# Attention with two feed-forward layers on one core: the probabilities of units 6 to 17 transposed by VectorE instead of TensorE

## The chip, the core and the metric

One core of a Trainium2 chip runs the whole program. The rows call the engines PE (TensorE's matmuls), PEld (its weight loads), DVE (VectorE), ACT (ScalarE), POOL (GpSimd) and SP (SyncE, which issues the DMAs here). The metric is the device time of one execution in microseconds; the time of a kernel is the median of its runs.

## The reference

Local attention over chunks of 64 tokens (8 batches, 8 heads, 576 tokens, head size 64), and two feed-forward layers on the 4608 tokens that come out:

```
scores = q_c @ k_c^T / 8                  # per head and chunk: 64 x 64
attn   = softmax(scores)
out    = attn @ v_c                       # then laid out as x: 4608 x 512
h      = (x @ w1) * (x @ w2) @ w3
y      = h @ w_out                        # 4608 x 512
g      = y @ w_in;  g = max(g,0) + alpha*min(g,0)
result = g @ w_out2                       # 4608 x 512
```

Everything is float32 on the outside. Inside, the large matmuls run in a 32-bit format with fewer bits (fp32r): each operand is split into a high and a low half, and three matmuls (`mm3`) replace one.

## The kernel before

The 4608 tokens are 9 blocks `b` of 512. A **unit** `u` is the attention of 256 tokens, so two units make the x of one block: 18 units. Four steps make a unit: `attn_scores` with `attn_max` and `attn_exp` (TensorE, VectorE, ScalarE); `attn_softmax` (VectorE scales the exponentials `e`); `attn_transpose` and `attn_copy` (TensorE transposes eight 128 x 128 tiles of `e` into the PSUM tile `pa`, ScalarE copies them to `pt` in SBUF); `attn_values` and `attn_out` (TensorE multiplies by the values, again into `pa`, and ScalarE and VectorE split the result into the halves of x).

The program has these stages. In the *first* the units 0 to 5, the conversion of the weights and the first projections of three blocks run in an order written out as a table. In the *second*, 24 steps `proj_wc` for blocks 0 to 2 follow each other, one per `f` of 8 and block: 12 matmuls `acc<-gs,wc` each, for which `load_g` fetches a product `g` from DRAM and VectorE and ScalarE split it into `gs` (three buffers). Units 6 and 7 are put between the steps by the dictionary `todo`. At the last `f` of a block `empty_pair` copies the accumulators to `y` (VectorE and ScalarE in turn) and stores them. In the *third*, blocks 3 to 8 are worked through in eight columns `f` each: `proj1` into bank `a`, `proj1` into bank `b`, and `proj_wc` of the column before into `acc`, 12 matmuls each. ScalarE copies `a` out of its bank, and VectorE's `product` (rows a<-b,a) multiplies it with bank `b`; the split makes `gs`. There is one bank of each kind. In blocks 3 to 7 the two units of the next block are put between the columns, a first unit at f = 0 to 3 and a second at 4 to 7; in blocks 3 to 6 a piece of the weights of the last stage is converted too (rows with m, p, raw, wm). The *last* stage, the second feed-forward layer, takes the rest of the time.

TensorE's order is the program's order in all stages. In the second and third stage the order on VectorE and ScalarE is set by a scheduler from the order of the code and from its own estimates.

Of the kernel before, what the change touches and what calls it, by code (L numbers as in the profile page):

```python
# [10 lines left out]
F32 = mybir.dt.float32  # L11
# [6 lines left out]
P = 128  # L18
# [34 lines left out]
LEAD = 3  # L53
# [6 lines left out]
def tile_attention_moe_moe(ctx: ExitStack, tc: tile.TileContext, qkv: bass.AP, w12: bass.AP,  # L60
# [14 lines left out]
    D = 64  # L75
# [7 lines left out]
    work = ctx.enter_context(tc.tile_pool(name="work", bufs=2))  # L83
# [25 lines left out]
    pe, act, dve = InOrder(nc.tensor), InOrder(nc.scalar), InOrder(nc.vector)  # L109
# [6 lines left out]
    def tmp(name):  # L116
        return work.tile([P, TB], F32, tag="tmp", name=name, bufs=TMP)
# [9 lines left out]
    def bank(which):  # L127
        return psum.tile([P, TB], F32, tag=which, name=which, bufs=1)

    def pair(which, name):  # L130
        return psum.tile([P, 2, TB], F32, tag=which, name=name, bufs=1)
# [64 lines left out]
    def convert():  # L196

        i = ahead[0]
        if i < len(conv):
            convert_a(i)  # L200
            convert_b(i)
            convert_c(i)
            convert_a(i + 1)
            convert_d(i)
            convert_e(i)
            ahead[0] = i + 1

    def w2_load(f):
        for half in range(2):
            g = w2_g[f, half] = granule(2 * f + half, "w2")  # L210
            nc.sync.dma_start(out=g.bitcast(F32), in_=w2_dram[f, half])
# [10 lines left out]
    un = {}  # L222
# [12 lines left out]
    def load_unit(u):  # L235
        unit_tiles(u)
        load_qk(u)
        load_v(u)
# [16 lines left out]
    def attn_scores(u, where="att"):  # L255
        s = un[u]["s"] = pair(where, "sc")
        for j in range(2):
            q, k = (un[u]["qk"][j][:, i].rearrange("p (a c s) -> p a c s", a=4, c=2) for i in range(2))
            for a in range(4):
                for h2 in range(2):  # L260
                    for c in range(2):
                        r0, c0, to = D * h2, D * c, (4 * j + a) * D
                        pe.matmul(s[c0:c0 + D, h2, to:to + D], q[r0:r0 + D, a, c], k[r0:r0 + D, a, c],
                                         start=True, stop=True)

    def attn_max(u):
        mx = un[u]["mx"] = small.tile([P, 2, 8], F32, tag="mx", name="mx")
        dve.tensor_reduce(out=mx, in_=un[u]["s"].rearrange("p h (a k) -> p h a k", k=D), axis=AX.X, op=ALU.max)
        dve.tensor_scalar_mul(mx, mx, -SCALE)

    def attn_exp(u, tiles=range(2)):
        mx, s, e = un[u]["mx"], un[u]["s"], un[u]["e"]
        if tiles[0] == 0:
            un[u]["sm"] = small.tile([P, 2, 4, 2], F32, tag="sm", name="sm")
        sm = un[u]["sm"]
        for j in tiles:
            for a in range(4):
                for h2 in range(2):
                    n, h = 4 * j + a, h2 ^ (a & 1 if u >= CROSS else 0)
                    act.activation(out=e[:, j, a, h], in_=s[:, h2, n * D:(n + 1) * D], func=AF.Exp,  # L280
                                         bias=mx[:, h2, n:n + 1], scale=SCALE, accum_out=sm[:, j, a, h:h + 1])

    def attn_softmax(u):
        e, sm = un[u]["e"].rearrange("p j a h k -> p (j a h) k"), un[u].pop("sm").rearrange("p j a h -> p (j a h)")
        dve.tensor_scalar_add(sm, sm, 1e-9)
        dve.reciprocal(sm, sm)
        dve.tensor_tensor(out=e, in0=e, in1=sm.unsqueeze(2).to_broadcast([P, 16, D]), op=ALU.mult)

    def attn_transpose(u, where="att"):
        e = un[u]["e"]  # L290
        pa = un[u]["pa"] = pair(where, "pa")
        for j in range(2):
            for a in range(4):
                pe.transpose(pa[:, j, a * P:(a + 1) * P], e[:, j, a].rearrange("p h k -> p (h k)"), ident)

    def attn_copy(u):
        pt = un[u]["pt"] = work.tile([P, 2, 4, 2, D], F32, tag="pt", name="pt", bufs=1)
        act.copy(pt.rearrange("p j a c s -> p j (a c s)"), un[u]["pa"])

    def attn_values(u):  # L300
        v, pt = un[u]["v"].rearrange("p j a (c d) -> p j a c d", c=2), un[u]["pt"]
        xo = un[u]["pa"].rearrange("p o (i j c s) -> p o i j c s", i=2, j=2, c=2)
        for j in range(2):
            for c in range(2):
                for i in range(2):
                    for odd in range(2):
                        for h2 in range(2):
                            a, h = 2 * i + odd, h2 ^ (odd if u >= CROSS else 0)
                            r, to = slice(D * h, D * h + D), slice(D * h2, D * h2 + D)
                            pe.matmul(xo[to, odd, i, j, c], v[r, j, a, c], pt[r, j, a, c], start=True, stop=True)  # L310

    def attn_out(u, lo):
        b, i = divmod(u, 2)
        if not lo and i == 0:
            x_t[b] = work.tile([P, 2, KD, TB], F32R, tag="x", name="x", bufs=2)
        xs = [x_t[b][:, s].rearrange("p (i o) t -> p o i t", o=2)[:, :, :, 2 * P * i:2 * P * (i + 1)] for s in (HI, LO)]
        pa = un[u]["pa"].rearrange("p o (i t) -> p o i t", i=2)
        if lo:
            dve.tensor_tensor(out=xs[LO], in0=pa, in1=xs[HI].bitcast(F32), op=ALU.subtract)
            un.pop(u)  # L320
        else:
            act.copy(xs[HI], pa)
# [23 lines left out]
    def proj1(b, f, which, ps):  # L346
        w = w_g["a", f, which].rearrange("p s (k c) -> p s k c", k=KD)
        for k in range(KD):
            mm3(ps, lambda s: w[:, s, k], lambda m: x_t[b][:, m, k], k == 0, k == KD - 1)

    def product(b, f, a, ps):
        dve.tensor_tensor(out=a, in0=ps, in1=a, op=ALU.mult)
        if b < LEAD:
            nc.sync.dma_start(out=g_dram[b, f], in_=a)
        else:
            split_g(b, f, a)
# [27 lines left out]
    def load_y(b, i):  # L384
        if i == 0:
            x_t[b, 2] = work.tile([P, 2, KD, TB], F32R, tag="x", name="y", bufs=2)
        raw = work.tile([P, 2, TB], F32, tag="raw", name="yraw", bufs=RAW)
        nc.sync.dma_start(out=raw, in_=y_dram[b][:, 2 * i:2 * i + 2])
        split(x_t[b, 2][:, :, 2 * i:2 * i + 2], raw)
# [33 lines left out]
    for step in STARTUP.split():  # L423
# [20 lines left out]
        elif kind == "k":  # L444
            a = ab[tuple(rest)][2] = tmp("a")
# [3 lines left out]
        elif kind == "m":  # L449
            _, ps, a = ab.pop(tuple(rest))  # L450
# [9 lines left out]
    def unit_steps(u, cut):  # L460


        def first():
            attn_scores(u)
            attn_max(u)
            attn_exp(u, range(1 if cut else 2))

        def second():
            if cut:
                attn_exp(u, range(1, 2))  # L470
            attn_softmax(u)
            if u + 1 < NU:
                load_unit(u + 1)

        def third():
            attn_transpose(u)
            attn_copy(u)

        def fourth():
            attn_values(u)  # L480
            attn_out(u, False)
            attn_out(u, True)
        return [first, second, third, fourth]
# [4 lines left out]
    load_unit(2 * LEAD)  # L488
    todo = {}
    for i in range(2):  # L490
        for at, part in zip((1, 3, 7, 9), unit_steps(2 * LEAD + i, True)):
            todo[10 * i + at] = part
    for n, (b, f) in enumerate(steps):
        if n + 2 < len(steps):
# [7 lines left out]
    for b in range(LEAD, NB):  # L502
        parts = [p for i in range(2) for p in unit_steps(2 * (b + 1) + i, False)] if b + 1 < NB else []
        for f in range(NF1):
            if parts and f % 4 == 1:
                parts[4 * (f // 4) + 1]()
            pa, pb = bank("a"), bank("b")
            proj1(b, f, 0, pa)
            a = tmp("a")
            act.copy(a, pa)  # L510
            if parts and f % 4 == 0:
                parts[4 * (f // 4)]()
            if parts and f % 4 == 2:
                parts[4 * (f // 4) + 2]()
            proj1(b, f, 1, pb)
            product(b, f, a, pb)
            if parts and f % 4 == 2:
                parts[4 * (f // 4) + 3]()
            if b < NB - 2:
                convert()  # L520
            if b == NB - 1:
                if f < 4:
                    w2_load(f)
                w2_load(4 + f)
                if f in (3, 6):
                    load_y(0, f // 3 - 1)
            proj_wc(*pend)
            pend = b, f
# [62 lines left out]
```

## Time and profile before

| | |
|---|---|
| median of 3 runs | 1518.82 us (1518.38 to 1521.39) |
| profiled execution | 1517.93 us, span 1516.2 us |
| TensorE busy | 1489.0 us, 98% of the span |
| VectorE busy | 792.7 us, 52% |
| ScalarE busy | 420.8 us, 28% |
| granted clock of TensorE | 1.00 throughout |

The second stage runs from about 224 to 298 us of the span, the third from there to about 805 us. A row of the timeline has its start, its length and, in brackets, how long the engine was idle before it and what ended that. Starts of successive rows of an engine say more than lengths, since instructions overlap.

### The profile page before, as it was taken

The numbers are of one execution on the slowest core, as the hardware profiler recorded it, in microseconds if no ns is written. First come the engines' busy times: TensorE is split into PE (matmuls) and PEld (weight loads), VectorE is DVE, ScalarE is ACT, GpSimd is POOL, SyncE is SP. The second block draws the span as 40 slices with busy tenths as digits, with TensorE's granted clock in tenths as the row PEclk, the third lists the DMA queues.
The fourth block names the chain that finished last, engine by engine and source line by source line (L and its number), as shares of the span: only waits on it lengthen the run. The fifth ranks groups of instructions, "written<-read, shape, count | busy, mean of one in ns | idle before, by whom it ended". The sixth has DMA issues, their size and how long they took to land.

```text
span 1516.2 us, 21102 instructions
## 1 busy us (share of the span) xinstructions
PE 1489.0 (98%) x8688; PEld 1228.1 (81%) x8688; DVE 792.7 (52%) x1250; ACT 420.8 (28%) x1108; POOL 0.7 (0%) x6
## 2 busy tenths in 40 slices
PE   5999999999999999999999999999999999999998
PEld 5778887788888888888888888888888888888887
DVE  7998983376666664221434343443434344343433
ACT  6553334344444443321111111111111111111111
POOL 0000000000000000000000000000000000000000
PEclk9999999999999999999999999999999999999999
DMA  8544457255555545156301010010101000000000
GB/s 304 164 139 151 148 165 224 87 198 166 182 183 175 181 163 185 43 166 195 112 0 56 0 43 14 3 53 1 56 0 56 1 14 28 1 28 0 29 1 28
DMA packets 61712, 141.89 MB, mean 94 GB/s; under 512 B 6576, under 2 KB 20912, under 8 KB 61616
## 3 DMA queue, kind: packets, MB, share of 16 engines
q1 hardware_dynamic: 61616, 140.54, 27.9%
q8 instruction: 68, 1.11, 0.3%
q14 instruction: 28, 0.23, 0.0%
HBM read 98.57 MB, written 41.94 MB: 93 GB/s over the span
## 4 chain that ended last, share of the span: by engine, by line
PE 90%; DVE 5%; ACT 2%; DMA 1%; issue 1%; SPq 0%; DVEq 0%; ACTq 0%
PE acc L104 38%; PE b L104 23%; PE a L104 22%; PE ab L104 2%; DVE m L104 2%; PE pa L104 2%; PE wc L104 2%; ACT e L104 1%; DVE p L104 1%; PE sc L104 1%; DMA g<-g_dram 1%; DMA raw<-in_w 0%; DVE a L104 0%; DVE e L104 0%; DVE w L104 0%
## 5 line engine op out<-in xcount | busy, mean ns | idle before, releaser
L104 PE MATMUL acc<-w,gs 128*128 128x512 f32 x1728 | 414.7, 389 | 0.0
L104 PEld LDWEIGHTS acc<-w,gs 128*128 128x128 f32 x1728 | 324.6, 188 | 67.0
L104 ACT CAST gs<-g 128x512 fp32r<-128x512 f32 x168 | 104.5, 622 | 661.3 <-DVE g L104 635.0
L104 PE MATMUL acc<-gs,wc 128*128 128x512 f32 x864 | 208.8, 393 | 3.1 <-DVE gs L104 3.0
L104 PE MATMUL a<-y,w 128*128 128x512 f32 x864 | 207.5, 389 | 0.0
L104 PE MATMUL b<-y,w 128*128 128x512 f32 x864 | 207.5, 389 | 0.0
L104 PEld LDWEIGHTS acc<-gs,wc 128*128 128x128 f32 x864 | 160.5, 188 | 39.3 <-DVE gs L104 4.2
L104 PEld LDWEIGHTS a<-y,w 128*128 128x128 f32 x864 | 162.3, 188 | 33.6
L104 PEld LDWEIGHTS b<-y,w 128*128 128x128 f32 x864 | 162.3, 188 | 33.6
L104 DVE TENSOR_TENSOR gs<-g,gs 128x512 fp32r<-128x512 f32 x168 | 116.2, 692 | 132.8 <-ACT gs L104 132.6
L104 PE MATMUL b<-x,wa 128*128 128x512 f32 x720 | 175.7, 393 | 0.1
L104 PE MATMUL a<-x,wa 128*128 128x512 f32 x720 | 173.5, 390 | 1.4 <-DVE x L104 1.4
L104 PEld LDWEIGHTS a<-x,wa 128*128 128x128 f32 x720 | 134.9, 188 | 29.6 <-DVE x L104 1.6
L104 PEld LDWEIGHTS b<-x,wa 128*128 128x128 f32 x720 | 133.6, 188 | 28.0 <-DVE wa L104 0.5
L104 DVE TENSOR_SCALAR g<-b,alpha_sb 128x512 f32<-128x512 f32 x72 | 54.0, 750 | 178.0 <-PE b L104 178.0
L104 DVE TENSOR_SCALAR g<-a,alpha_sb 128x512 f32<-128x512 f32 x72 | 54.0, 751 | 162.3 <-PE a L104 162.3
L104 ACT ACTIVATE e<-sc,mx 128x64 f32<-128x64 f32 x288 | 85.7, 354 | 29.0 <-DVE mx L104 28.9
L104 DVE TENSOR_SCALAR m<-m 128x512 f32<-128x512 f32 (+1 forms) x144 | 60.9, 424 | 59.9 <-ACT m L104 58.3
L104 DVE TENSOR_TENSOR a<-b,a 128x512 f32<-128x512 f32 x60 | 41.3, 688 | 88.1 <-PE b L104 84.0
L104 ACT COPY a<-a 128x512 f32<-128x512 f32 x60 | 35.9, 599 | 138.7 <-PE a L104 119.9
L104 PE MATMUL ab<-x,wa 128*128 128x512 f32 x288 | 68.4, 392 | 2.7 <-ACT a L104 2.7
L104 ACT ACTIVATION_READ_ACCUMULATOR e<-sc,mx 128x1 f32 x288 | 70.5, 248 | 0.0
(55 smaller groups left out, 978.6 us busy)
## 6 DMA issues: line engine op xcount, KB each, us to landing
qk<-in_qkv SPq DMA_DIRECT2D x36, 512.0 KB, 6.2
raw<-in_w2nd SPq DMA_DIRECT2D x32, 512.0 KB, 4.1
w_dram<-wm SPq DMA_DIRECT2D x32, 512.0 KB, 3.2
w<-w_dram SPq DMA_DIRECT2D x32, 512.0 KB, 4.3
y_dram<-y SPq DMA_DIRECT2D x36, 256.0 KB, 3.0
yraw<-y_dram SPq DMA_DIRECT2D x18, 512.0 KB, 4.3
out<-o SPq DMA_DIRECT2D x36, 256.0 KB, 2.1
raw<-in_w SPq DMA_DIRECT2D x16, 512.0 KB, 4.2
```

Of the source, the lines that this page charges most:

```text
L104: ins = op(*args, **kw)
```

## The change

From unit 6 on, `attn_transpose` and `attn_copy` are replaced by `attn_transpose_blocks`: 16 VectorE transposes of 32 partitions by 8 x 32 elements each, from `e` straight into `pt`. Each turns eight 32 x 32 blocks and places them in the partition group where `attn_values` reads them. `pa` is now used by the values alone. In the second stage the third part moves from step 7 to 4 (and 17 to 14). In the third stage it moves from after `a` of column 2 to the start of column 1, right behind the scaling, and the values move from the end of column 2 to after `a` of column 3 (in the second unit from 6 to 7).

```diff
+    def attn_transpose_blocks(u):
+
+        e = un[u]["e"]
+        un[u]["pa"] = pair("att", "pa")
+        pt = un[u]["pt"] = work.tile([P, 2, 4, 2, D], F32, tag="pt", name="pt", bufs=1)
+        B = D // 2
+        for c in range(2):
+            for i in range(2):
+                for h in range(2):
+                    for k in range(2):
+                        r, to = B * (2 * c + i), B * (2 * h + k)
+                        dve.transpose(out=pt[to:to + B, :, :, c, B * i:B * i + B].rearrange("p j a s -> p (j a) s"),
+                                      in_=e[r:r + B, :, :, h, B * k:B * k + B].rearrange("p j a s -> p (j a) s"))
...
         def third():
-            attn_transpose(u)
-            attn_copy(u)
+            attn_transpose_blocks(u)
...
-        for at, part in zip((1, 3, 7, 9), unit_steps(2 * LEAD + i, True)):
+        for at, part in zip((1, 3, 4, 9), unit_steps(2 * LEAD + i, True)):
             todo[10 * i + at] = part
...
             if parts and f % 4 == 1:
                 parts[4 * (f // 4) + 1]()
+                parts[4 * (f // 4) + 2]()
             pa, pb = bank("a"), bank("b")
             proj1(b, f, 0, pa)
             a = tmp("a")
             act.copy(a, pa)
             if parts and f % 4 == 0:
                 parts[4 * (f // 4)]()
-            if parts and f % 4 == 2:
-                parts[4 * (f // 4) + 2]()
+            if parts and f % 4 == 3:
+                parts[4 * (f // 4) + 3]()
             proj1(b, f, 1, pb)
             product(b, f, a, pb)
-            if parts and f % 4 == 2:
-                parts[4 * (f // 4) + 3]()
```

On TensorE, from column 2 of a block of the third stage on (sc are the scores, pa<-ident,e the transposes, pa<-pt,v the values), before:

```order
L104 MATMUL a<-x,wa 128x512 x12
L104 MATMUL pa<-ident,e 128x128 x8
L104 MATMUL b<-x,wa 128x512 x12
L104 MATMUL pa<-pt,v 64x64 x32
L104 MATMUL acc<-gs,wc 128x512 x12
L104 MATMUL a<-x,wa 128x512 x12
L104 MATMUL b<-x,wa 128x512 x12
L104 MATMUL acc<-gs,wc 128x512 x12
L104 MATMUL a<-x,wa 128x512 x12
L104 MATMUL sc<-qk 64x64 x32
```

and now:

```order
L104 MATMUL a<-x,wa 128x512 x12
L104 MATMUL b<-x,wa 128x512 x12
L104 MATMUL acc<-gs,wc 128x512 x12
L104 MATMUL a<-x,wa 128x512 x12
L104 MATMUL pa<-pt,v 64x64 x32
L104 MATMUL b<-x,wa 128x512 x12
L104 MATMUL acc<-gs,wc 128x512 x12
L104 MATMUL a<-x,wa 128x512 x12
L104 MATMUL sc<-qk 64x64 x32
```

The transposes are gone, and the values stand one column later, between `a` and `b`.

On VectorE, at the first unit of block 5, from the scaling of `e` on, before:

```order
L104 TENSOR_TENSOR e<-e,sm 128x1024
L104 TENSOR_SCALAR p<-m 128x512
L104 TENSOR_SCALAR m<-m 128x512
L104 SCALAR_TENSOR_TENSOR p<-raw,p 128x512
L104 TENSOR_TENSOR a<-b,a 128x512
L104 TENSOR_TENSOR m<-m,wm 128x512
L104 TENSOR_SCALAR m<-m 128x512
L104 TENSOR_TENSOR gs<-a,gs 128x512
```

and now:

```order
L104 TENSOR_TENSOR e<-e,sm 128x1024
L104 TENSOR_SCALAR p<-m 128x512
L104 STREAM_TRANSPOSE pt<-e 32x8x32 x16
L104 TENSOR_TENSOR a<-b,a 128x512
L104 SCALAR_TENSOR_TENSOR p<-raw,p 128x512
L104 TENSOR_TENSOR m<-m,wm 128x512
L104 TENSOR_TENSOR gs<-a,gs 128x512
```

The 16 transposes stand ahead of the product a<-b,a, and two convert steps that stood ahead of it moved behind it.

On VectorE, at unit 7 in the second stage, before:

```order
L104 TENSOR_TENSOR e<-e,sm 128x1024
L104 TENSOR_TENSOR gs<-g,gs 128x512 x2
L104 COPY y<-acc 128x512 x2
L104 TENSOR_TENSOR gs<-g,gs 128x512 x4
L104 TENSOR_TENSOR x<-pa,x 128x2x2x256
```

and now:

```order
L104 TENSOR_TENSOR e<-e,sm 128x1024
L104 TENSOR_TENSOR gs<-g,gs 128x512
L104 STREAM_TRANSPOSE pt<-e 32x8x32 x16
L104 TENSOR_TENSOR gs<-g,gs 128x512
L104 COPY y<-acc 128x512 x2
L104 TENSOR_TENSOR gs<-g,gs 128x512 x4
L104 TENSOR_TENSOR x<-pa,x 128x2x2x256
```

The transposes stand ahead of one `gs` and of the two copies that empty the accumulators.

## Rows read from the trace of the kernel before

**Rows 1.** The page's busy times and shares of the span.
```profile
PE 1489.0 (98%) x8688; PEld 1228.1 (81%) x8688; DVE 792.7 (52%) x1250; ACT 420.8 (28%) x1108; POOL 0.7 (0%) x6
```

**Rows 2.** Stretches: length, PE, PEld, DVE, ACT, POOL, clock, DMA share, GB/s.
```profile
200.00:300.00 100.00, 97.18 (x664) 78.32 (x663) 47.74 (x77) 37.11 (x108) 0.00 (x0) 1.00 0.54 169
400.00:500.00 100.00, 100.00 (x746) 82.38 (x745) 66.12 (x118) 45.38 (x148) 0.00 (x0) 1.00 0.52 172
```

**Rows 3.** Waits of PE after 200 us: total, times, longest.
```profile
PE acc L104 <- DVE gs L104: 3.0, 3, 1.8
```

**Rows 4.** Groups by line and form: busy us, mean ns of one.
```profile
L104 DVE TENSOR_TENSOR a<-b,a 128x512 f32<-128x512 f32 x60 | 41.3, 688 | 88.1 <-PE b L104 84.0 <-issue 4.2
...
L104 PE MATMUL pa<-ident,e 128*128 128x128 f32 x144 | 19.5, 282 | 4.3 <-DVE e L104 4.3
L104 ACT COPY pt<-pa 128x1024 f32<-128x1024 f32 x18 | 18.4, 1020 | 8.1 <-PE pa L104 8.0
```

**Rows 5.** Timeline of PE, block 4: four starts of bank a.
```profile
387.85 2.89 PE L104 MATMUL a<-x,wa 128*128 128x512 f32 x12
...
398.22 2.88 PE L104 MATMUL a<-x,wa 128*128 128x512 f32 x12
...
406.38 2.88 PE L104 MATMUL a<-x,wa 128*128 128x512 f32 x12
...
415.86 2.88 PE L104 MATMUL a<-x,wa 128*128 128x512 f32 x12
```

**Rows 6.** Timeline of DVE, block 3: successive convert steps.
```profile
347.92 0.42 DVE L104 TENSOR_SCALAR m<-m 128x512 f32<-128x512 f32 x1
348.26 0.69 DVE L104 SCALAR_TENSOR_TENSOR p<-raw,p 128x512 f32<-128x512 uint32 x1
348.86 0.69 DVE L104 TENSOR_TENSOR m<-m,wm 128x512 f32<-128x512 f32 x1
```

**Rows 7.** Timeline, block 5, first unit.
```profile
455.45 1.22 DVE L104 TENSOR_TENSOR e<-e,sm 128x1024 f32<-128x1024 f32 x1
...
456.58 0.42 DVE L104 TENSOR_SCALAR p<-m 128x512 uint32<-128x512 uint32 x1
456.99 0.43 DVE L104 TENSOR_SCALAR m<-m 128x512 f32<-128x512 f32 x1
...
462.92 1.03 PE L104 MATMUL pa<-ident,e 128*128 128x128 f32 x8
```

**Rows 8.** Timeline, block 4, second unit: first row behind scaling and gs.
```profile
419.94 0.42 DVE L104 TENSOR_SCALAR p<-m 128x512 uint32<-128x512 uint32 x1
...
426.74 1.03 PE L104 MATMUL pa<-ident,e 128*128 128x128 f32 x8
```

**Rows 9.** Timeline, block 3, first unit.
```profile
313.37 0.43 DVE L104 TENSOR_SCALAR m<-m 128x512 f32<-128x512 f32 x1
...
318.23 1.03 PE L104 MATMUL pa<-ident,e 128*128 128x128 f32 x8
```

**Rows 10.** Timeline, second stage, unit 6.
```profile
238.63 0.69 DVE L104 TENSOR_TENSOR gs<-g,gs 128x512 fp32r<-128x512 f32 x1
...
244.57 1.03 PE L104 MATMUL pa<-ident,e 128*128 128x128 f32 x8
```

**Rows 11.** Timeline, second stage, unit 7.
```profile
269.74 0.69 DVE L104 TENSOR_TENSOR gs<-g,gs 128x512 fp32r<-128x512 f32 x1
...
275.06 0.59 ACT L104 COPY y<-acc 128x512 f32<-128x512 f32 x1 [0.77 <-DVE y L104]
276.05 4.97 SPq L371 DMA_DIRECT2D g<-g_dram  x6
...
282.81 3.01 PE L104 MATMUL acc<-gs,wc 128*128 128x512 f32 x12 [1.81 <-DVE gs L104]
```

**Rows 12.** Timeline, block 7, first unit.
```profile
599.20 1.22 DVE L104 TENSOR_TENSOR e<-e,sm 128x1024 f32<-128x1024 f32 x1
...
607.61 1.03 PE L104 MATMUL pa<-ident,e 128*128 128x128 f32 x8
```

## The prediction

> **What bounds the kernel now.** I read the page first. TensorE is busy for 1489.0 of 1516.2 us, VectorE for just over half of the span [rows 1]. In the stretches, TensorE is full from 300 us on at a granted clock of 1.00 (the upper level, 2.4 GHz), while VectorE is 66% busy in 400 to 500 us; only between 200 and 300 us does TensorE have gaps, 2.8 us of them [rows 2]. The waits of TensorE after 200 us agree: one kind is left, the halves `gs` from VectorE, 3.0 us in three places [rows 3]. So in the third stage each instruction taken from TensorE shortens the kernel by its time, as long as VectorE goes on delivering in time. The forecast therefore needs three things: what the transposes take on TensorE, what they take on VectorE, and how late VectorE may be at each place where they now stand.
>
> **Taken from TensorE.** Eight transposes for each of 12 units; the list's row holds 144 for 18 units, at 282 ns each [rows 4], but those overlap, so I take starts in the timeline. A column of the third stage (a, b, acc: 36 matmuls) lasts 406.38 - 398.22 = 8.16 us; one with scores between a and b lasts 415.86 - 406.38 = 9.48; one with transposes and values lasts 398.22 - 387.85 = 10.37 [rows 5]. The values are 64 matmuls of the scores' shape and will now stand where the scores stand, between a and b, so I price them like the scores: the transposes of a unit are 10.37 - 9.48 = 0.89 us. Ten units of the third stage give 8.9 us. The copy pt<-pa, 18 times 1.02 us [rows 4], leaves ScalarE, which TensorE did not wait for there; I count it at nothing, and if ScalarE were the limit it would be a further gain.
>
> **Added to VectorE.** 16 instructions per unit, each of 32 partitions by 256 elements. No such operation is in the trace. Neighbours: an instruction that takes 512 elements in 256 steps lasts 0.42 us and the next begins 0.34 us after it; one of 512 steps lasts 0.69 and the next begins after 0.60 [rows 6]. So 256 steps without a wait between them come every 0.34 us: the lower bound, 5.4 us a unit. If neighbours don't overlap, 0.42 us: 6.7 us a unit, the upper bound. An operation that turns a 32 by 32 block can't put out its first row before 32 elements came in; from 512 to 1024 elements the distance grows from 0.60 [rows 6] to 456.58 - 455.45 = 1.13 us [rows 7], 1.04 ns an element, so up to 0.03 us more than the lower bound. I take **0.36 us, D = 5.76 us a unit**, near the lower end because 15 of the 16 wait for nothing. The rest of this part is worked out in D, since everything hangs on it.
>
> The Trainium skill, "VectorE: DVE Perf Modes", section "The DRAIN you can't avoid", says that the next operation doesn't start until the pipe of the one before is empty, and its rules advise a small number of instructions. Rows 6 show starts closer than durations, by 0.08 to 0.09 us, so this trace doesn't agree for those kinds; by that rule D would be the upper bound.
>
> **What waits behind them, third stage.** VectorE works in order. Behind the 16 transposes stands the product a<-b,a of the unit's second column, which frees bank b for the next column. It lasts 0.69 us [rows 4], and I add 0.06 for the signal, an assumption, so it must begin 0.75 us before TensorE wants bank b.
> - First unit of a block (blocks 4 to 6): the transposes begin where a convert step began at 456.99; TensorE, with no transposes of its own, wants the bank at 462.92, the end of a [rows 7]. Room: 5.93 - 0.75 = 5.18 us.
> - First unit of block 3: VectorE gets there later against TensorE: 318.23 - 313.37 - 0.75 = 4.11 us [rows 9].
> - Second unit (blocks 3 to 6): 426.74 - 419.94 - 0.75 = 6.05 us [rows 8].
> - Block 7 has no conversion: the scaling begins at 599.20 and its successor 1.13 later, the bank is due at 607.61 [rows 12]: 6.53 us; the second unit is looser.
>
> With D = 5.76 TensorE waits 1.65 us in block 3, and 0.58 three times: 3.4 us together; the second units and block 7 wait for nothing. Behind the product stand convert steps and the next `gs`, with about 1 us of room, and they move together with the late TensorE. Third stage: -8.9 + 3.4 = **-5.5 us**.
>
> **What waits behind them, second stage.** Units 6 and 7 stand among steps of 12 matmuls, 2.72 us each, where VectorE must deliver one `gs` per step. Here a burst of 5.8 us covers two steps.
> - Unit 6: the last `gs` ahead of the burst begins at 238.63, so the burst runs from 239.23 to 244.99 and the `gs` behind it is usable 0.75 later, 245.74. It is due where unit 6's own transposes stood before, at 244.57 [rows 10]. The step waits 1.17 us; the 0.89 us of those transposes fall away: **+0.28 us**.
> - Unit 7: the `gs` at 269.74, then the burst from 270.34 to 276.10, one more `gs`, and only then the copies y<-acc that empty the accumulators of block 1. The first begins at 276.70, VectorE's second 0.60 later and ends at 277.99, and ScalarE's last, 0.03 behind it and 0.59 long, at 278.61, where before it ended at 275.06 + 0.59 = 275.65 [rows 11]. SyncE issues the stores of these copies and, queued behind them, the loads of g (276.05); the wait of 1.81 us for `gs` at 282.81 comes from those loads [rows 11]. So the whole chain moves by 2.96 us, and the transposes taken away ahead of it only lengthen that wait: **+2.96 us**, with no credit.
>
> Second stage: +3.2 us. Sum: -5.5 + 3.2 = **-2.3 us**. The profiled execution took 1517.93 us (span 1516.2 and 1.7 around it), 0.9 under the median of 1518.82. From the median: **1516.5 us**. In D (second stage, gain, block 3, three first units, four second units, block 7): 5.4 gives 2.5 - 8.9 + 1.3 + 0.7 = -4.4; 6.1 gives about 0; 6.4 gives +3.0; 6.72 gives 5.2 - 8.9 + 2.6 + 4.6 + 2.7 + 0.2 = +6.4.
>
> About 0.2%, 3 us, is what a measurement of this kernel can tell from no change. That is D below 5.6 for faster, above 6.4 for slower.
>
> **The rivals.**
> - *The gain stays* (chance 0.33). The transposes come every 0.34 us or less. For it: 15 of 16 have no wait, and rows 6 have this distance. Then -4.4 us, 1514.4; if moreover the copies y<-acc of unit 7 are not held up (2.6 us), 1512.
> - *The late product* (0.29), on the other side. If a transpose costs 0.40 us or more, every unit with conversion makes TensorE wait for bank b: at 0.42 us 1.5 us in each first unit, 0.7 in each second, 2.6 in block 3, and 5.2 in the second stage: 1518.8 + 6.4 = 1525.2. The change turns at 0.38 us. For it: durations without overlap, and nothing in the trace shows how this operation overlaps with itself. Against it: all other kinds do overlap. The rule of the Trainium skill's VectorE page named above gives this case.
> - *Two steps per element* (within the 0.29, 0.04 of it): 0.60 us as for the 512-step rows, D = 9.6: 10.9 - 8.9 + 5.5 + 13.3 + 14.2 + 6 = +41 us, 1560. Outside the range.
>
> The Trainium skill's "Vector Engine (DVE) Microarchitecture Reference", section 3.8, says that the transposing front end sustains one element per cycle and lane; no run here shows it yet, and it speaks against the last case.
>
> **How the numbers follow.** The forecast, a result within 3 us of before, has 0.38, the two others 0.33 and 0.29. Faster 0.33, same 0.38, slower 0.29. The range goes from 1512 (gain stays and no hold-up in unit 7) to 1526 (the upper bound of 0.42 us and a little): outside are the case of 0.60 us, 0.04, prices between 0.43 and 0.60, some 0.07, and a gain above 7 us, some 0.07. The likeliest case's own range is 1515.8 to 1521.8, two sides of 1518.8.
>
> **What would show it.** Right: the column with the values lasts 9.5 us; transposes 0.35 to 0.37 us apart; TensorE waits for VectorE's a in the first units only, 0.6 us (block 3: 1.6), and for the copies y<-acc near 275 us some 3 us; the wait behind them is still there. Wrong: no waits on bank b (then D is below 5.2 or the scaling ends earlier), waits in second units too (D above 6.05), or TensorE waiting for x at a block's start: in the second unit the values now end only 5.44 us (b and acc) ahead of the next block's a, and x<-pa,x stands behind some 4.7 us of convert steps; I left it some 1.5 us of room, the thinnest place of the working.

## The result and the profile after

The changed kernel takes 1536.98 us (median of 4 runs, 1535.05 to 1538.32) against 1518.6 for the kernel before beside it: ratio 1.0116, 95% interval 1.0104 to 1.0128. It is 18.4 us slower, outside the range of the forecast and beyond its slower rival. The profiled execution took 1536.36 us with a span of 1534.6.

The page's busy times, which answer to [rows 1]:

```profile
PE 1487.7 (97%) x8592; PEld 1221.4 (80%) x8592; DVE 869.7 (57%) x1442; ACT 408.7 (27%) x1096; POOL 0.7 (0%) x6
```

The stretches, in the columns of [rows 2]:

```profile
200.00:300.00 100.00, 91.97 (x619) 73.60 (x618) 60.52 (x108) 35.18 (x106) 0.00 (x0) 0.95 0.54 169
300.00:400.00 100.00, 96.15 (x715) 78.19 (x713) 77.20 (x151) 41.33 (x143) 0.00 (x0) 1.00 0.48 158
400.00:500.00 100.00, 94.92 (x759) 76.67 (x758) 82.43 (x159) 39.35 (x116) 0.00 (x0) 0.98 0.52 171
500.00:600.00 100.00, 95.32 (x685) 77.07 (x687) 81.23 (x160) 41.48 (x141) 0.00 (x0) 0.98 0.47 155
```

TensorE has lost its 96 transposes and is nevertheless longer under way: it is no longer full between 200 and 600 us, and its granted clock is below 1.00 in three of the four stretches. TensorE's waits after 200 us (total, times, longest), against the one row of [rows 3]:

```profile
PE b L104 <- DVE a L104: 14.3, 9, 2.9
PE acc L104 <- ACT y L104: 5.2, 1, 5.2
PE acc L104 <- DVE gs L104: 3.0, 2, 2.7
```

The first two rows are new: bank b, which VectorE's product must free, nine times, and the accumulators, once. The reason stands in one row of the groups (busy us, mean ns of one, idle before):

```profile
L104 DVE STREAM_TRANSPOSE pt<-e 32x256 f32<-32x256 f32 x192 | 83.6, 436 | 2.5
```

and in the timeline of block 5's first unit, the place of [rows 7]:

```profile
469.75 0.42 DVE L104 TENSOR_SCALAR p<-m 128x512 uint32<-128x512 uint32 x1
470.09 7.18 DVE L104 STREAM_TRANSPOSE pt<-e 32x256 f32<-32x256 f32 x16
...
473.42 2.88 PE L104 MATMUL a<-x,wa 128*128 128x512 f32 x12
477.30 0.69 DVE L104 TENSOR_TENSOR a<-b,a 128x512 f32<-128x512 f32 x1
...
478.05 3.02 PE L104 MATMUL b<-x,wa 128*128 128x512 f32 x12 [1.75 <-DVE a L104]
...
480.91 2.88 PE L104 MATMUL acc<-gs,wc 128*128 128x512 f32 x12
```

From the first of 16 transposes to the end of the last are 7.18 us, so they come (7.18 - 0.436) / 15 = 0.450 us apart, more than their own length of 0.436: they don't overlap at all. The product behind them begins at 477.30, and TensorE, which had ended a, gets bank b at 478.05. The row says 1.75 us of waiting. Counted in starts it is more: a to b 478.05 - 473.42 = 4.63 where 2.72 would do, and b to acc 2.86 instead of 2.72, 2.05 us in all. The other waits for bank b cost 0.29 to 0.33 us beside what their rows say too, apart from two behind which the clock was down.

The second stage, unit 7, the place of [rows 11]:

```profile
272.81 0.68 DVE L104 TENSOR_TENSOR gs<-g,gs 128x512 fp32r<-128x512 f32 x1
273.41 7.17 DVE L104 STREAM_TRANSPOSE pt<-e 32x256 f32<-32x256 f32 x16
...
280.61 0.69 DVE L104 TENSOR_TENSOR gs<-g,gs 128x512 fp32r<-128x512 f32 x1
281.22 1.28 DVE L104 COPY y<-acc 128x512 f32<-128x512 f32 x2
...
282.58 10.21 PE L104 MATMUL acc<-gs,wc 128*128 128x512 f32 x36 [5.21 <-ACT y L104]
283.92 3.05 SPq L385 DMA_DIRECT2D g<-g_dram  x6
```

The copies y<-acc stand behind the burst, TensorE waits for empty accumulators, and the loads of g come after that. Around this wait the clock is down (length, PE busy and matmuls, clock, DMA share, GB/s):

```profile
276.00:280.00 4.00, 1.36 (x7) 0.94 0.00 0
280.00:284.00 4.00, 1.42 (x3) 0.50 0.32 115
284.00:288.00 4.00, 4.00 (x14) 0.71 1.04 255
288.00:292.00 4.00, 4.00 (x20) 1.00 0.78 289
```

A clock of 0.50 is the lower of the two levels, 1.2 GHz; in the slice after it, at 0.71 in the mean, TensorE is busy throughout and gets through 14 matmuls in 4 us, against 20 at 1.00.

The starts of the third stage's first projection and of the last stage's, before and then now:

```profile
297.86 2.88 PE L104 MATMUL a<-x,wa 128*128 128x512 f32 x12
728.17 2.88 PE L104 MATMUL a<-y,w 128*128 128x512 f32 x12
```

```profile
304.83 2.88 PE L104 MATMUL a<-x,wa 128*128 128x512 f32 x12
746.60 2.88 PE L104 MATMUL a<-y,w 128*128 128x512 f32 x12
```

So the third stage ended near 728 us before, not near 805 as said above; nothing in the argument hangs on that. Up to the third stage 7.0 us were lost, 0.3 of them before the second stage began. The third stage lasts 441.77 us instead of 430.31, 11.5 more. The last stage lasts 788.0 us in both.

### The profile page after: what moved, and what is told of

The parts are those of the page before. It is cut to its first block, busy times and chain, and to the rows that moved or that the text cites. A ratio compares the mean times of both kernels' runs of the same rounds, so it can differ in the third digit from the quotient of the medians.

```text
span 1534.6 us, 21067 instructions
## 1 busy us (share of the span) xinstructions
PE 1487.7 (97%) x8592; PEld 1221.4 (80%) x8592; DVE 869.7 (57%) x1442; ACT 408.7 (27%) x1096; POOL 0.7 (0%) x6
## 4 chain that ended last, share of the span: by engine, by line
PE 73%; DVE 15%; ACT 5%; DMA 3%; issue 2%; SPq 1%; ACTq 0%; DVEq 0%
PE acc L104 32%; PE b L104 18%; PE a L104 17%; DVE pt L104 5%; ACT e L104 4%; DVE m L104 3%; PE ab L104 2%; DVE p L104 2%; PE wc L104 2%; PE pa L104 1%; DVE mx L104 1%; DVE e L104 1%; DMA v<-in_qkv 1%; DVE a L104 1%; DVE gs L104 1%
## 5 line engine op out<-in xcount | busy, mean ns | idle before, releaser
L104 PEld LDWEIGHTS acc<-gs,wc 128*128 128x128 f32 x864 | 163.8, 191 | 45.3 <-ACT y L104 6.1
L104 PE MATMUL b<-x,wa 128*128 128x512 f32 x720 | 180.4, 400 | 14.5 <-DVE a L104 14.3
L104 DVE STREAM_TRANSPOSE pt<-e 32x256 f32<-32x256 f32 x192 | 83.6, 436 | 2.5
L104 ACT ACTIVATION_READ_ACCUMULATOR e<-sc,mx 128x1 f32 x288 | 70.5, 248 | 0.0
```

What stands on the lines that cost most here:

```text
L104: ins = op(*args, **kw)
```

## Experiments

The theory: the transposes cost 0.45 us instead of 0.36, and the two places where a whole burst stands ahead of something that TensorE needs, product and accumulator copies, turn that into waits. Rivals: the later values make x late; VectorE has simply too much to do; or the loss of one stage drives the other.

**The values' new place alone.** TensorE transposes as before, the values move to column 3:

```diff
                 parts[4 * (f // 4) + 2]()
+            if parts and f % 4 == 3:
+                parts[4 * (f // 4) + 3]()
             proj1(b, f, 1, pb)
             product(b, f, a, pb)
-            if parts and f % 4 == 2:
-                parts[4 * (f // 4) + 3]()
```

> The kernel before, with TensorE's transposes kept at column 2 of the third stage and only the values and the split of x moved to after a of column 3. Theory (the loss is VectorE's burst of 16 transposes, 0.45 us apart where 0.36 was taken): no change, 1518.6 within 2 us, no wait of TensorE for x at a block's start. Rival (the later values make x late for the next block, four or five blocks by 1 to 2 us each): 1522 to 1528, with waits of bank a for x.

Measured: 1519.3 us, ratio 1.0001 (0.9992 to 1.001). No wait for x and none for bank b, and the third stage lasts 430.32 us as before. The new place costs nothing.

**One stage at a time.** First the third stage only, with units 6 and 7 at their old steps, then the second stage only (the condition turned, and the third stage's order as before):

```diff
         def third():
-            attn_transpose_blocks(u)
+            if cut:
+                attn_transpose(u)
+                attn_copy(u)
+            else:
+                attn_transpose_blocks(u)
```

> The changed kernel, with units 6 and 7 in the second stage transposed by TensorE as before. Theory (two separate losses, one of about 7 us in the second stage, one of about 11 in the third, by the starts of block 3 in the two traces, 304.83 against 297.86): about 1530, block 3 begins at 297.9, the nine waits for bank b stay. Rival (the loss of the second stage drives the third, by what it shifts): 1519 or below.

Measured: 1527.44 us, ratio 1.0051 (1.0036 to 1.0066), with nine waits for bank b, 13.0 us together. Nearer the theory's 1530 than the rival's 1519.

> The kernel before, with only units 6 and 7 in the second stage transposed by VectorE. Theory: about 1525.6 (7.0 us later at block 3, nothing after it). Rival (the loss is all in the third stage and the second's is made up behind it): 1518.6.

Measured: 1525.13 us, ratio 1.0039 (1.0026 to 1.0051); the third stage begins at 305.18 and is undisturbed. So each stage loses by itself, 9.2 and 6.9 us. Their sum is 2.3 us short of 18.4. In the profiles the missing part lies in the third stage: alone it has one clock drop and waits of 1.73 or 1.74 us in the first units of blocks 4 to 6, in the changed kernel two drops and 2.35, 1.75 and 2.70. Whether the late second stage causes this was not tried.

**Four wide transposes instead of sixteen.** The placing across partition groups is left out:

```diff
-        for c in range(2):
-            for i in range(2):
...
+        for h in range(2):
+            for k in range(2):
+                dve.transpose(out=pt[:, :, :, h, B * k:B * k + B].rearrange("p j a s -> p (j a) s"),
+                              in_=e[:, :, :, h, B * k:B * k + B].rearrange("p j a s -> p (j a) s"))
```

> The changed kernel with 4 transposes of 128 partitions in place of 16 of 32; each turns its blocks within their own partition group, so the probabilities go to wrong places: the placing across partition groups is left out. Same elements per partition and instruction. Theory (the price is per instruction, the same 0.45 us, so a unit's burst is 1.8 us and inside every room): all waits for bank b vanish, the gain of 8.9 us in the third stage and about 0.9 in the second remain: 1508.8, from 1507 to 1511. Rival 1 (the price goes by partitions or elements in all, 1.8 us an instruction): 1537 as the changed kernel. Rival 2 (the transposes on TensorE were covered by something else, and taking them away gives nothing): 1518.

Measured: 1508.01 us, ratio 0.9924 (0.9909 to 0.9939). In the timeline of VectorE, first unit of block 5:

```profile
450.46 1.41 DVE L104 STREAM_TRANSPOSE pt<-e 128x256 f32<-128x256 f32 x4
451.80 0.65 DVE L104 TENSOR_TENSOR a<-b,a 128x512 f32<-128x512 f32 x1
```

The burst is 1.41 us, no wait for bank b or for y is left, and 10.2 us are gained. The third stage lasts 421.37 us (from 295.04 to 716.41), 8.9 less than before, which is what the prediction took from TensorE; the rest lies in the second stage. So the time taken from TensorE was sized right, and all of it is to be had. Unexpected: these four are (451.80 - 450.46) / 4 = 0.335 us apart, not 0.45. The price per instruction isn't the same.

**The same work, spread out.** All 16 transposes, units 6 and 7 by TensorE, but in four groups:

```diff
                 parts[4 * (f // 4) + 1]()
-                parts[4 * (f // 4) + 2]()
+                parts[4 * (f // 4) + 2]((0,))
+            if parts and f % 4 == 2:
+                parts[4 * (f // 4) + 2]((2,))
...
             product(b, f, a, pb)
+            if parts and f % 4 in (1, 2):
+                parts[4 * (f // 4) + 2]((2 * (f % 4) - 1,))
```

> Third stage of the change with the same 16 transposes per unit, issued as four groups of four (start of column 1, behind its product, start of column 2, behind its product); units 6 and 7 by TensorE as before. In VectorE's order 4 (first unit) or 6 (second unit) transposes now stand ahead of the product a<-b,a in place of 16. Theory (the loss is where the burst stands, 1.8 or 2.7 us against rooms of 4.1 to 6): no wait for bank b, the whole gain of 8.9 us: 1509.3, from 1508 to 1511. Rival (the loss is VectorE's total of 7.2 us more per unit, so it falls behind wherever the transposes stand): 1517 to 1527, with waits for bank b, for gs or for x.

Measured: 1512.73 us, ratio 0.9961 (0.9949 to 0.9974), with a profiled execution of 1510.29. No wait for bank b; one for x, 0.55 us. The median lies above the expected 1508 to 1511.

**One call moved.** The transposes are issued behind the product of column 1 instead of ahead of it, all 16 at once; the scheduler puts 3 or 6 of them ahead of the product by itself:

```diff
                 parts[4 * (f // 4) + 1]()
-                parts[4 * (f // 4) + 2]()
...
             product(b, f, a, pb)
+            if parts and f % 4 == 1:
+                parts[4 * (f // 4) + 2]()
```

> As the changed kernel in the third stage with one call moved: the transposes are issued behind the product of column 1 and not ahead of it; units 6 and 7 by TensorE. The scheduler puts 3 (first unit) or 6 (second unit) ahead of the product, 3 more ahead of the next gs, the rest behind. Theory: as with four groups, 1509.3, from 1508 to 1511, since neither product nor gs is late. Rival (total load): 1517 to 1527.

Measured: 1509.08 us, ratio 0.9939 (0.9926 to 0.9952): the best version that computes the reference, and faster than both kernels. In VectorE's order, first unit of block 5:

```profile
452.21 0.42 DVE L104 TENSOR_SCALAR p<-m 128x512 uint32<-128x512 uint32 x1
452.55 1.32 DVE L104 STREAM_TRANSPOSE pt<-e 32x256 f32<-32x256 f32 x3
453.90 0.69 DVE L104 TENSOR_TENSOR a<-b,a 128x512 f32<-128x512 f32 x1
454.62 1.33 DVE L104 STREAM_TRANSPOSE pt<-e 32x256 f32<-32x256 f32 x3
455.99 0.69 DVE L104 TENSOR_TENSOR gs<-a,gs 128x512 fp32r<-128x512 f32 x1
456.71 4.53 DVE L104 STREAM_TRANSPOSE pt<-e 32x256 f32<-32x256 f32 x10
```

TensorE waits for neither bank b nor x in the third stage, although VectorE is fuller than in the changed kernel (77 and 82% in these stretches):

```profile
300.00:400.00 100.00, 100.00 (x791) 81.95 (x784) 89.02 (x174) 45.99 (x151) 0.00 (x0) 1.00 0.53 175
400.00:500.00 100.00, 100.00 (x734) 82.07 (x732) 86.00 (x167) 43.19 (x145) 0.00 (x0) 1.00 0.53 173
```

The same instructions at the same price gain 9.0 us or lose 9.2, by what stands ahead of what. The rival of too much work on VectorE falls.

**Spread in the second stage too**, a group at each of steps 4 to 7 and 14 to 17:

```diff
+        for q in range(4):
+            todo[10 * i + 4 + q] = lambda third=parts[2], q=q: third((q,))
```

> The four groups in the third stage, and in the second stage too, one group at each of steps 4 to 7 and 14 to 17. Theory: unit 6 gains its 0.9 us; at unit 7 about 8 transposes still stand ahead of the copies y<-acc, which are 1.5 to 2 us late, and the loads of g behind them too: 1509.3 - 0.9 + 1.7 = 1510.1, from 1508 to 1512, not better than leaving units 6 and 7 to TensorE. Rival (spread transposes cost nothing there either): 1507.5.

Measured: 1512.15 us, ratio 0.9963 (0.9948 to 0.9978), not to be told from 1512.73. TensorE waits for the copies y<-acc in both blocks:

```profile
250.36 3.02 PE L104 MATMUL acc<-gs,wc 128*128 128x512 f32 x12 [2.54 <-ACT y L104]
...
277.17 5.73 PE L104 MATMUL acc<-gs,wc 128*128 128x512 f32 x24 [1.75 <-ACT y L104]
```

I had expected one such wait, at unit 7; the groups are late for the copies at unit 6 too. Spread in this way the transposes gain nothing in that stage. The wide ones, with a burst of 1.41 us, did: it lasted 70.5 us there, against 72.7 to 74.1 in the profiles where TensorE transposes units 6 and 7.

**What a transpose costs.** Five runs of the changed kernel with other instructions, one execution each. First every transpose cut into halves of 32 by 128:

```diff
+                        for j in range(2):
+                            dve.transpose(out=pt[to:to + B, j, :, c, B * i:B * i + B],
+                                          in_=e[r:r + B, j, :, h, B * k:B * k + B])
```

> The changed kernel with each transpose cut into two of 32 partitions by 128 elements, so 32 instructions per unit and the same elements. Theory (a price per instruction of 0.45 us that is 0.18 fixed and 1.04 ns per element): 0.32 us apart, a burst of 10.1 us, and a time of 1560 to 1575. Rival (the price goes by elements alone, as for a slow rate): 0.22 us apart, a burst of 7.2 us, 1537.

Measured: 1553.53 us and a burst of 8.14 us for 32, (8.14 - 0.28) / 31 = 0.254 us apart. Neither theory. The 0.196 us between 0.254 and 0.450 is no price of 128 elements, since the halves come in pairs on the same partitions, and the starts alternate, 0.24 and 0.27 us apart; the runs below say what that means.

Then transposes that stay in their own partition group (the placing is left out; the first diff), and, apart from that, the loops of the changed kernel turned (h and k outside, c and i inside, every block in its right place):

```diff
-                        dve.transpose(out=pt[to:to + B, :, :, c, B * i:B * i + B].rearrange("p j a s -> p (j a) s"),
+                        dve.transpose(out=pt[r:r + B, :, :, h, B * k:B * k + B].rearrange("p j a s -> p (j a) s"),
```

> The changed kernel with 16 transposes of 32 partitions by 256 elements that stay in their own partition group (the placing is left out, so the probabilities go to wrong places). Theory A (crossing from one partition group to another is what makes a transpose 0.45 us, since with 128 partitions that stay in place 4 took 1.41 us, 0.33 apart): 0.335 apart, a burst of 5.4 us, about 1514 to 1518. Theory B (working on 32 partitions is what costs): 0.45 apart as in the changed kernel, 1537.

> The changed kernel with the loops turned: successive transposes now write the same 32 partitions at different columns, where before they wrote other partitions at the same columns. Theory C (an instruction waits for the one before it because both write the same columns): 0.335 apart, 1514 to 1518. Theories A and B: 0.45 apart, 1537.

Measured without crossing, first unit of block 5, and with the loops turned:

```profile
461.82 5.71 DVE L104 STREAM_TRANSPOSE pt<-e 32x256 f32<-32x256 f32 x16
467.56 0.69 DVE L104 TENSOR_TENSOR a<-b,a 128x512 f32<-128x512 f32 x1
```

```profile
436.32 7.18 DVE L104 STREAM_TRANSPOSE pt<-e 32x256 f32<-32x256 f32 x16
```

Without crossing they are (467.56 - 461.82) / 16 = 0.359 us apart; with the loops turned still 0.45. The first looks like theory A, but two things don't fit it: in the changed kernel 4 of the 16 stay in their group and are no cheaper (shortest 425 ns, longest 442), and without crossing the starts are not even: 0.32 to 0.33 within a group, 0.40 to 0.41 and then 0.37 where every fourth goes on to the next group. The times: 1520.08 us against 1520.34 beside it, where I expected 1514 to 1518 (in this one execution the second stage began at 226.78 us, 3.0 later than in the profile of before); waits of 4.1 us for bank b, 3.7 for y and 2.3 for gs are left, and the clock is 0.94 between 270 and 300 us. And 1540.43 us with the loops turned.

So a fourth theory, D: what counts is whether an instruction works on the same partition groups as the one before it. Two runs take crossing and change apart: own group, but another one each time (the loops of h and k outside); and every one crossing, with four in a row from one group to the same other:

```diff
-                        r, to = B * (2 * c + i), B * (2 * h + k)
+                        r, to = B * (2 * c + i), B * (2 * c + 1 - i)
```

> Transposes that stay in their own partition group, as in the run without crossing, but with the loops turned, so that each works on another group than the one before it (placing left out). In the run without crossing the group changed at every fourth; there the starts were 0.33 us apart within a group and 0.40 where the group changed. Theory A (crossing costs, a change of group a little): 0.40 apart, a burst of 6.4 us. Theory D (a change of group from one instruction to the next is the whole cost, and two groups changing is no more): 0.45 apart, 7.2 us. Theory A without the change: 0.33, 5.4 us.

> Every one of the 16 crosses to the neighbouring partition group, and four in a row go from the same group to the same group (placing wrong, so the probabilities are in wrong places). Theory A (crossing costs): 0.40 to 0.45 apart throughout, a burst of 6.4 to 7.2 us. Theory D (the change of group is the cost): 0.33 apart within four, 0.45 between, a burst of 5.8 us.

Measured, first without crossing but with a change each time, then with crossing in fours:

```profile
436.46 7.18 DVE L104 STREAM_TRANSPOSE pt<-e 32x256 f32<-32x256 f32 x16
```

```profile
459.43 5.72 DVE L104 STREAM_TRANSPOSE pt<-e 32x256 f32<-32x256 f32 x16
```

7.18 us without any crossing, 5.72 with nothing but crossing. Theory A falls, D stands: crossing is free, and 0.45 us is the price of a transpose whose neighbours use other partitions. No transpose but the first of a burst waits for another VectorE instruction by a semaphore in these traces, so it isn't the program that holds them apart. The halves fit as well: if a change costs them 0.450 - 0.326 = 0.124 us too, a half without a change comes every 0.19 us, and the 128 elements more of a whole one cost 1.05 ns each, an estimate from these distances that is near the 1.04 of [rows 6] and [rows 7]. Of the whole kernels the first took 1539.96 us and the second 1516.82, beside 1520.95.

## Why the prediction was wrong

**The step that failed** is "I take 0.36 us, D = 5.76 us a unit", together with its upper bound of 0.42. Measured: 0.45, D = 7.2. The rows from which I took both ends are of instructions that all use the same partitions as the one before. In this change every transpose writes another partition group than the one before it, and then nothing overlaps. That 0.36 is also the mean of transposes that change group at every fourth is a coincidence: the prediction came to it from 0.34 and the filling of a block. I had written that nothing in the trace shows how this operation overlaps with itself, and then still let the longest duration of another operation be the end of the range. My argument against the slower price, that all other kinds overlap, was a misreading too: in the trace of before an instruction that reads what the one ahead of it wrote begins after that one's end,

```profile
397.81 0.42 DVE L104 TENSOR_SCALAR p<-m 128x512 uint32<-128x512 uint32 x1
398.26 0.69 DVE L104 SCALAR_TENSOR_TENSOR p<-raw,p 128x512 f32<-128x512 uint32 x1
```

0.45 us apart at a length of 0.42. The rule of the Trainium skill, "VectorE: DVE Perf Modes", section "The DRAIN you can't avoid", that the next operation waits for the pipe of the one before to empty, agrees with the transposes of the changed kernel (0.450 apart, 0.436 long). The same paragraph goes on that a next operation that isn't held starts earlier (which ones are held it leaves to another section); the prediction left that half out. The wide transposes, which all use the same 128 partitions (0.335 apart, 0.410 long), and [rows 6] are of that kind by their starts.

**The rooms in the third stage were right.** With D = 7.18 put into the prediction's own working, block 3 waits 3.1 us, the other first units 2.0 each, the second units 1.1 each, and block 7 1.1 in all: 14.7 us. Measured: 14.3 in nine waits, and 0.1 in a tenth. Unit 6 of the second stage: 239.23 + 7.18 + 0.75 - 244.57 = 2.6 us against 2.70. Two runs had nearly the prediction's own D: the transposes without crossing 5.71 us, those that cross in fours 5.72. There TensorE waits for bank b just in the four first units that the prediction names, 4.1 and 3.7 us where it worked out 3.4, and the third stage is 3.6 and 3.9 us shorter than before where it worked out 5.5. The 0.75 us from the product to bank b, in part an assumption, came out as well (477.30 to 478.05). So the mechanism was right in the third stage, and the price was wrong.

**What was left out.** By the working, D = 7.18 gives +11.9 us (6.1 in the second stage, 14.7 - 8.9 = 5.8 in the third). Measured were 18.4. In the third stage the ten waits are 14.4 us by their rows, and the 0.3 us that each costs beside its row make 3.1. And the clock: behind two of them the 12 matmuls of b ran at the lower level, for instance

```profile
402.70 4.44 PE L104 MATMUL b<-x,wa 128*128 128x512 f32 x12 [2.35 <-DVE a L104]
406.98 2.90 PE L104 MATMUL acc<-gs,wc 128*128 128x512 f32 x12
```

4.28 us from b to acc where 2.86 are usual, 1.4 us each, 2.8 together. 14.4 + 3.1 + 2.8 - 8.9 = 11.4 of the third stage's 11.5. The prediction had no term for the clock and none for the 0.3 us.

In the second stage the clock is down behind both long waits as well and takes some 3 us, an estimate: 24 matmuls from 247.67 to 255.26 last 7.59 us, the next 24 last 6.02; 36 from 282.58 last 10.14, the next 48 last 11.02. In return the waits for `gs` that the kernel before had there, 0.89 and 1.81 us, are gone. The prediction had said that the 1.81 behind the copies would stay, so that its 6.1 comes near the 7.0 is luck in part.

**The terms that held.** 0.89 us of transposes per unit: the column with the values lasts 455.78 - 446.30 = 9.48 us, as forecast, and the wide version gains the whole. ScalarE's copy was free: with it gone, the wide version's third stage gains no more than TensorE's 8.9. x was never late in the changed kernel, the thinnest place of the working; in the spread version, with its 0.55 us, it is the next to give.

**The chances.** The slower rival was named with its mechanism, place and turning point of 0.38 us, and had 0.29; prices between 0.43 and 0.60 us, where 0.45 lies, had some 0.07. It was the right story with a price too low. The sign named for a price that is too low, waits in the second units too, is in the rows.

## What to carry to other kernels

Work taken from a full engine is worth its time only if the engine that takes it over isn't in front of the first one's next operand: ask, for each burst, which instruction stands behind it and how long its reader can wait. Here one call moved by a few lines turned a loss of 9 us into a gain of 9. When an operation isn't in the trace, bounds from other operations are no bounds for it, neither its length nor whether it overlaps with itself: measure it, or let the range say so; and once the bottleneck waits, count the clock and the restart too.

## What the hardware did that I had not expected

In these runs successive VectorE transposes overlap only when source and target are in the partition groups of the one before. With 32 partitions by 256 float32 elements the starts are 0.33 us apart within one pair of groups, 0.45 when source or target changes every time, and 0.36 on average when they change at every fourth; the halves of 128 elements, two in a row on the same groups, had 0.254. Whether source or target changes made no difference, and moving blocks to another group cost nothing by itself. Where another VectorE operation, on all 128 partitions, stands beside a transpose, the rows look alike: a transpose from the first group to the first overlaps with the operation ahead of it, unless that one wrote what it reads (469.75 and 470.09 above, 0.34 apart at a length of 0.42), while in the profiles of the changed kernel, of the four groups and of the one call moved no other transpose overlaps with such an operation, at either side (454.62 begins 0.72 after a product of 0.69; 477.30 after the end of the burst; both in rows above). So it may be the first partition that counts; two operations that aren't transposes, on different groups, were not tried.

TensorE's clock fell to the lower level behind waits of 2.35, 2.70, 2.70 and 5.21 us in the profile of the changed kernel, but not behind one of 2.87 us at 328.22 there, while in the version with the third stage alone it fell behind an equal one:

```profile
322.36 4.61 PE L104 MATMUL b<-x,wa 128*128 128x512 f32 x12 [2.87 <-DVE a L104]
```

So the length of the wait alone doesn't decide it; what does was not tried.
